# Keys of batches 1 to 3 by stationary sketches in 64x32 tiles, turned in PSUM, with their sums and copies on VectorE

## The chip, the cores and the metric

The kernel runs on one core of a Trainium2 chip. The metric is the device time of one execution in microseconds (us). Nine runs of the kernel before have a median of 267.28 us (266.45 to 270.02). One execution was also profiled: it took 267.74 us, of which the profile's span covers 265.9 us, with TensorE's clock granted in full throughout.

## The reference, cut to what matters

An attention block without softmax is followed by a two-layer network with an exact GELU. For keys and queries, two sketch matrices S1 and S2 (8x32 each) give two vectors of 8 numbers per token, and the features are their outer product, 64 numbers.

```python
def phi(x):
    a = np.einsum('rd,bhsd->bhsr', S1, x)
    b = np.einsum('rd,bhsd->bhsr', S2, x)
    return np.einsum('bhsi,bhsj->bhsij', a, b).reshape(*x.shape[:-1], r * r)
q_p, k_p = (phi(q), phi(k))
kv = np.einsum('bhsf,bhsd->bhfd', k_p, v)
z = np.sum(k_p, axis=2)
num = np.einsum('bhsf,bhfd->bhsd', q_p, kv)
den = np.einsum('bhsf,bhf->bhs', q_p, z)[..., None] + 1e-06
x = num / den            # then heads side by side: 4352 tokens of 128 channels
out = gelu(x @ w_in) @ w_out        # 128 -> 2048 -> 128
```

There are 4 batches, 4 heads, 1088 tokens and a head width of 32. All is float32. Of the tokens of a head, 1024 are the main part and 64 are the remainder.

## The kernel before, in words

The tokens are worked through in chunks: two of 512 tokens per batch (n = 0 to 7) and a last one that holds the 64 remaining tokens of all batches. A chunk needs its batch's `kv` and `z`, so the keys of a whole batch are done ahead of its first chunk. Batch 0 is done at the start, in its own way (`key_features`, `kv_first`), and isn't touched by the diff.

The body is a list of steps, one hidden tile (128 of the 2048 hidden channels of one chunk) per step. In step t, TensorE does the hidden tile (`hidden`, L697), ScalarE its GELU (L704), and TensorE the products with `w_out` of earlier steps (`two_products`, L782). From the third block of chunk 0 on, these use sums of four hidden tiles that GpSimd makes (`token_sums`, L747 to L750: bits_low, bits_a, bits_e, bits_m) and sums of the columns of `w_out` (`channel_sums`, L734 to L737). When a chunk is done, ScalarE and VectorE read its two banks (`drain`, L794 to L803), VectorE combines them (`combine`, L816 to L819), turns the result (L845) and SP stores it.

All other work is hung into steps by hand with `at(t, f, ...)`. Within a step the order is: drains, the hidden tile, token sums, the functions hung there, stores, products. A final loop fixes the order of the text on every engine, so each engine works strictly in that order, and an instruction that waits holds up all behind it on its engine.

For batches 1 to 3 the keys go like this. SP loads a batch's keys with 16 transfers (`load_turned_k`, L108) and its values with one (L100); SP issues all transfers in the order of the text. VectorE turns the keys in blocks of 32x32 (`key_turn_blocks`, L353), two steps ahead of a chunk for batches 2 and 3 (step 30 for batch 2, 62 for batch 3) and at step 14 for batch 1. `features_of_all` has TensorE multiply (`key_products`, L368): blocks of 64 tokens are stationary and the sketches `S12` (32 columns) move, 32 products of 64x64 tiles per batch. ScalarE copies the first factor out of PSUM (`a_t`, L954). `outer_of_all` has VectorE make the features `k_p` (L964). `add_tokens` then adds features of different tokens (L413, L416), for batch 1 on GpSimd and for batches 2 and 3 on VectorE, and for batches 2 and 3 `add_last` adds once more and adds the remainder (L423, L424). `finish_keys` has TensorE make `kv` and `z` (`kv_sum`, L446): 32 products of features and values, 4 for the remainder, and for `z` products with a tile of ones: 4 for batches 2 and 3, and 12 for batch 1 (4 of these with `ones_rem`). These steps are 16, 17 and 21 for batch 1, 38 and 45 for batch 2, 69 and 77 for batch 3.

PSUM has eight banks: two for hidden tiles (`hps`), two for products with `w_out` (`ops`), and two pairs for everything else (`wps`, `work_banks`). A query chunk uses such a pair in the same way as the new keys: `query_sketch` (L584) multiplies stationary sketches in 64x32 tiles with 256 moving columns, and `query_outer` (L596 to L619) turns the result inside PSUM and goes on from there. `attend` (L633) has tiles of the same shape.

Of the kernel before, what the change touches and what calls it, by code (L numbers as in the profile page):

```python
# [8 lines left out]
FP = mybir.dt.float32  # L9
# [7 lines left out]
def kernel(  # L17
# [49 lines left out]
    def work_banks():  # L67

        return wps.tile([128, 2, CW], FP, name="w_ps")
# [4 lines left out]
    def halves(banks):  # L74
        return [banks[:, i] for i in range(2)]
# [23 lines left out]
    def load_main(eng, n, b, heads=slice(0, H)):  # L99
        eng.dma_start(out=main[n, b][:, heads],  # L100
                      in_=src_of[n][b, heads, 0:MAIN, :].rearrange("h (p j) d -> p h j d", j=J))

    def load_turned_k(b):

        src = k[b, :, 0:MAIN, :].rearrange("h (jj t pb jc) d -> h pb t jj (jc d)", jj=4, t=32, pb=4)
        for h in range(H):
            for pb in range(4):
                sp.dma_start(out=main["k", b][pb * 32:(pb + 1) * 32, h].rearrange("t (jj jc) d -> t jj (jc d)", jj=4),  # L108
                             in_=src[h, pb])

    def load_q(n):
        at = n % NCH * CW
# [85 lines left out]
    def load_rest():  # L198

        load_w_out(1, gated=True)  # L200
        for i in range(2, len(pieces)):
            load_w_in(i)
            load_w_out(i)
        for b in range(1, B):
            load_turned_k(b)
            load_main(sp, "v", b)
# [19 lines left out]
    kz_first = big.tile([128, 128], FP, name="kz_first")  # L226

    ones = big.tile([128, D], FP, name="ones")

    ones_rem = big.tile([128, D], FP, name="ones_rem")  # L230
    pool.memset(ones_rem, 0.0)
    pool.memset(ones_rem[:REM], 1.0)
# [113 lines left out]
    def key_turn(b, r, ps, copy, midway=lambda: None):  # L346
        kT[r] = transposed(ps, "kT", [four_tokens("k", b, h, c) for h in (r, r + 2) for c in range(NCH)], copy, midway)

    def key_turn_blocks(b, r):

        kT[r] = att.tile([128, CW], FP, name="kT")
        for i in range(2):
            dve.transpose(out=kT[r][:, i * 256:(i + 1) * 256].rearrange("p (jc jj t) -> p jj jc t", jc=2, jj=4),  # L353
                          in_=main["k", b][:, r + 2 * i].rearrange("p (jj jc) d -> p jj jc d", jj=4))

    def spread(out, a, b):

        n = a.shape[1]
        return dict(out=out, in0=a[:, :, :, None].broadcast_to([128, n, R, R]),
                    in1=b[:, :, None, :].broadcast_to([128, n, R, R]))  # L360

    def key_products(r, banks, col=0):

        for i in range(2 * NCH):
            for c in range(2):
                for t in range(2):
                    at = i * 128 + c * 64
                    pe.matmul(banks[t][c * 64:(c + 1) * 64, col + i * 32:col + (i + 1) * 32],  # L368
                              lhsT=kT[r][t * 64:(t + 1) * 64, at:at + 64],
                              rhs=S12[t * 64:(t + 1) * 64, 2 * t:2 * t + 2].rearrange("p h r -> p (h r)"),  # L370
                              start=True, stop=True)
# [33 lines left out]

    k_s = {}

    def add_tokens(b, r, eng):

        words = mlp.tile([128, LC], U32, name="bits_r")  # L410
        k_s[r] = words.bitcast(FP).rearrange("p (c two one f) -> p c two one f", c=NP, two=2, one=2)
        kp = k_p[b, r].rearrange("p t (c two one) i j -> p t c two one (i j)", c=NP, two=2)
        eng.tensor_add(out=k_s[r].rearrange("p c two one f -> p (c two one f)"),  # L413
                       in0=kp[:, 0].rearrange("p c two one f -> p (c two one f)"),
                       in1=kp[:, 1].rearrange("p c two one f -> p (c two one f)"))
        eng.tensor_add(out=k_s[r][:, :, 0], in0=k_s[r][:, :, 0], in1=k_s[r][:, :, 1])  # L416

    def add_last(b, eng):

        rows = slice(b // 2 * REM, (b // 2 + 1) * REM)  # L420
        for r in range(2):
            to = k_s[r][:, :, 0, 0]
            eng.tensor_add(out=to, in0=to, in1=k_s[r][:, :, 0, 1])  # L423
            eng.tensor_add(out=to[rows], in0=to[rows], in1=k_p_rem[b % 2][rows, r::2].rearrange("p c i j -> p c (i j)"))  # L424

    def flat(features):
        return features.rearrange("p i j -> p (i j)")

# [15 lines left out]
    def kv_product(ps, lhsT, features, h, part, start=False, stop=False):  # L444

        pe.matmul(ps[h * D:(h + 1) * D, part * F:(part + 1) * F], lhsT=lhsT, rhs=features, start=start, stop=stop,  # L446
                  skip_group_check=True)

    def kv_sum(b, ps):


        for i in range(J):
            ch, t, one = i % 2, i // 4, i // 2 % 2
            for h in range(H):
                kv_product(ps, main["v", b][:, h, i, :], flat(k_p[b, h % 2][:, t, h // 2 * 4 + ch * 2 + one]), h, 0,
                           start=i == 0)
# [20 lines left out]
        sketch_of_z(b, banks[:, 0], F)  # L477


    S_abc = [big.tile([128, 2, 2, 2 * R], FP, name=f"S_abc{b}") for b in range(B)]  # L480
    own_r = big.tile([128, 2], FP, name="own_r")

    def spread_sketches():

        pool.tensor_add(out=own_r, in0=mask4[:, 0:2], in1=mask4[:, 2:4])
        own = own_r[:, None, :, None]
        w = S_abc[0]
        pool.memset(w, 0.0)
        pool.tensor_mul(out=w[:, :, :, 0:4], in0=sT[:, 0:R].rearrange("p (i f) -> p i f", i=2)[:, :, None].broadcast_to([128, 2, 2, 4]),
                        in1=own.broadcast_to([128, 2, 2, 4]))  # L490
        pool.tensor_mul(out=w[:, :, :, R:], in0=sT[:, None, None, R:].broadcast_to([128, 2, 2, R]),
                        in1=own.broadcast_to([128, 2, 2, R]))
        for b in range(1, B):
            pool.tensor_copy(out=S_abc[b], in_=w)

# [443 lines left out]
    def at(t, f, *a):  # L939
        slots[t].append(lambda: f(*a))  # L940


    def features_of_all(b):
        banks = halves(work_banks())
        for r in range(2):
            key_products(r, banks, r * 128)
        held["keys"] = banks


        held["factors"] = []  # L950
        for r in range(2):
# [5 lines left out]
    def factors(bank, r):  # L957
        return bank[:, r * 128:(r + 1) * 128].rearrange("p (n r) -> p n r", r=2 * R)

    def outer_of_all(b, adds_by=dve):  # L960
        for r, a in enumerate(held["factors"]):
            k_p[b, r] = att.tile([128, 2, J, R, R], FP, name="k_p")
            for t in range(2):
                dve.tensor_mul(**spread(k_p[b, r][:, t], a[:, t, :, 0:R], factors(held["keys"][t], r)[:, :, R:2 * R]))  # L964
        for r in range(2):
            add_tokens(b, r, adds_by)

    held = {}

# [44 lines left out]
    for n in range(3, NCHUNK):  # L1014

        t = (n - 1) * NF
        b = (n + 1) // 2
        keys = n % 2 and b < B
        if n > 3:
            at(t - 6, query_turn, n)  # L1020
        at(t - 1, attend, n - 1)
        at(t - 1, query_sketch, n)
        at(t - 1, query_outer, n)
        if keys:
            for r in range(2):
# [128 lines left out]
```

## Time and profile before

| | |
|---|---|
| median of nine runs | 267.28 us |
| profiled execution | 267.74 us |
| span of its profile | 265.9 us |
| hidden tiles, L697 | 138.7 us of TensorE |
| GELU, L704 | 73.1 us of ScalarE |
| token sums, L747 to L750 | 143.6 us of GpSimd, 1.3 us each |
| key products of batches 1 to 3, L368 (192 instructions) | 3.4 us of TensorE |
| features of these keys, L964 (12) | 7.4 us of VectorE |
| sums of these keys on VectorE, L413, L416, L423, L424 (16) | 15.4 us |
| sums of batch 1's keys on GpSimd, L413, L416 (4) | 4.0 us |
| turns of these keys, L353 (12) | 4.2 us of VectorE |
| copies of the first factor, L954 (12) | 1.6 us of ScalarE |

Matmuls of TensorE overlap, and busy time counts instructions one by one. A float32 product is recorded as two instructions, so 32 products are x64 in a line of the profile. In the timeline a line gives the start, the length, the engine, the source line, the operation with its tiles, the count, and in brackets the idle time before it with what ended it. In the waits a line gives who waited for what, the sum, the times and the longest.

### The profile page before, as it was taken

To read this page: it belongs to the slowest core of one execution; us is meant where nothing else is said; L and a number is where in the kernel's file an instruction comes from. 1 tells how busy PE (TensorE), PEld (TensorE's weight loads), DVE (VectorE), ACT (ScalarE), POOL (GpSimd) and SP (SyncE) were. 2 spreads that over 40 slices of the span, in tenths; PEclk is the share of its full clock that TensorE was granted. 3 is DMA by queue.
4 is the path that set the end of the run, shared out by engine and by line. 5 is a ranking of instruction groups with operands and counts; after the bars stand their busy time and mean duration, and the time that the engine had idled before them with its cause. 6 is when DMAs were issued, how large, how long until landed. Compare 5 with 4: busy or idle time off the path is not lost.

```text
span 265.9 us, 6138 instructions
## 1 busy us (share of the span) xinstructions
PE 258.7 (97%) x2489; PEld 134.3 (50%) x2489; DVE 147.7 (56%) x315; ACT 118.3 (44%) x239; POOL 169.5 (64%) x180
## 2 busy tenths in 40 slices
PE   8799999999999999999999999999999999999995
PEld 6655444345445454444455554454444454445794
DVE  3776878428499996764085995570456033600140
ACT  5474777433623533353435334533353344433441
POOL 3513006899997875687767877687768776877200
PEclk9999999999999999999999999999999999999999
DMA  6489253525100201102000002002000100020021
GB/s 203 130 249 333 59 171 68 169 63 169 36 7 2 33 10 19 23 0 42 0 2 2 1 2 42 0 1 42 0 0 14 30 2 0 4 38 0 2 35 24
DMA packets 35756, 13.50 MB, mean 51 GB/s; under 512 B 28433, under 2 KB 34321, under 8 KB 35729
## 3 DMA queue, kind: packets, MB, share of 16 engines
q1 hardware_dynamic: 35536, 13.05, 19.5%
q8 instruction: 19, 0.31, 0.4%
q10 hardware_dynamic: 192, 0.07, 0.1%
q14 instruction: 9, 0.07, 0.1%
HBM read 10.88 MB, written 2.23 MB: 49 GB/s over the span
## 4 chain that ended last, share of the span: by engine, by line
PE 66%; SPq 14%; DMA 11%; DVE 6%; issue 2%; POOL 0%; ACT 0%; DVEq 0%; ACTq 0%
PE h_ps L697 31%; PE o_ps L782 28%; SPq L108 7%; DMA v<-in_v_dram 5%; DMA block<-in_moe_w_out_dram 4%; PE w_ps L830 3%; SPq L128 2%; DMA small<-in_moe_w_in_dram 2%; SPq L124 2%; PE w_ps L633 1%; PE w_ps L446 1%; PE w_ps L584 1%; SPq L169 1%; SPq L100 1%; DVE sums L819 1%
## 5 line engine op out<-in xcount | busy, mean ns | idle before, releaser
L697 PE MATMUL h_ps<-xT,w_in 128*64 128x512 f32 (+3 forms) x516 | 138.7, 576 | 0.0
L704 ACT ACTIVATE block<-h_ps 128x512 f32<-128x512 f32 (+1 forms) x128 | 73.1, 571 | 120.1 <-PE h_ps L697 115.8
L782 PE MATMUL o_ps<-block,w_out 128*64 128x256 f32 x224 | 57.8, 380 | 0.0
L697 PEld LDWEIGHTS h_ps<-xT,w_in 128*64 128x64 f32 (+1 forms) x516 | 42.1, 143 | 29.4 <-issue 10.6
L747 POOL TENSOR_TENSOR bits_low<-block 128x512 f32<-128x512 f32 x28 | 35.7, 1274 | 27.0 <-ACT block L704 27.0
L782 PEld LDWEIGHTS o_ps<-block,w_out 128*64 128x64 f32 x224 | 30.1, 137 | 38.7 <-issue 25.5
L748 POOL TENSOR_TENSOR bits_a<-block 128x512 f32<-128x512 f32 x28 | 35.7, 1277 | 13.0 <-ACT block L704 13.0
L749 POOL TENSOR_TENSOR bits_e<-bits_a,block 128x512 f32<-128x512 f32 x28 | 36.3, 1295 | 2.2
L750 POOL TENSOR_TENSOR bits_m<-block,bits_e 128x512 f32<-128x512 f32 x28 | 35.9, 1282 | 2.2
L782 PE MATMUL o_ps<-block,small 128*64 128x256 f32 x112 | 29.1, 383 | 0.6 <-DVE sums L798 0.6
L782 PE MATMUL o_ps<-bits_low,small 128*64 128x256 f32 x112 | 29.2, 383 | 0.0
L782 PE MATMUL o_ps<-bits_a,small 128*64 128x256 f32 x112 | 29.1, 382 | 0.0
L782 PE MATMUL o_ps<-bits_m,w_out 128*64 128x256 f32 x112 | 28.7, 379 | 0.0
L798 DVE TENSOR_TENSOR sums<-o_ps,sums 64x512 f32<-64x512 f32 x8 | 5.5, 682 | 41.6 <-ACT sums L795 24.0
L596 DVE STREAM_TRANSPOSE w_ps<-w_ps 128x512 f32<-128x512 f32 (+1 forms) x7 | 4.8, 686 | 40.6 <-PE w_ps L584 40.6
L782 PEld LDWEIGHTS o_ps<-block,small 128*64 128x64 f32 x112 | 14.7, 137 | 19.9 <-issue 10.3
L782 PE MATMUL o_ps<-bits_e,small 128*64 128x256 f32 x112 | 17.2, 385 | 0.6 <-POOL bits_e L749 0.6
L833 PE MATMUL o_ps<-g,w_out 128*128 128x512 f32 x32 | 16.4, 600 | 0.1
L782 PEld LDWEIGHTS o_ps<-bits_m,w_out 128*64 128x64 f32 x112 | 15.3, 137 | 0.0
L782 PEld LDWEIGHTS o_ps<-bits_a,small 128*64 128x64 f32 x112 | 14.8, 137 | 0.0
L782 PEld LDWEIGHTS o_ps<-bits_low,small 128*64 128x64 f32 x112 | 14.7, 137 | 0.0
L782 PEld LDWEIGHTS o_ps<-bits_e,small 128*64 128x64 f32 x112 | 7.4, 136 | 11.5 <-issue 8.5
(186 smaller groups left out, 307.0 us busy)
## 6 DMA issues: line engine op xcount, KB each, us to landing
block<-in_moe_w_in_dram SPq DMA_DIRECT2D x3, 512.0 KB, 8.1
block<-in_moe_w_out_dram SPq DMA_DIRECT2D x3, 512.0 KB, 10.9
k<-in_k_dram SPq DMA_DIRECT2D x48, 32.0 KB, 1.8
v<-in_v_dram SPq DMA_DIRECT2D x3, 512.0 KB, 4.2
q<-in_q_dram SPq DMA_DIRECT2D x24, 64.0 KB, 3.4
out_dram<-oT SPq DMA_DIRECT2D x24, 64.0 KB, 2.2
k<-in_k_dram SPq DMA_DIRECT2D x2, 256.0 KB, 3.0
q<-in_q_dram SPq DMA_DIRECT2D x2, 256.0 KB, 5.0
```

The lines of the kernel that those rows point to most:

```text
L108: sp.dma_start(out=main["k", b][pb * 32:(pb + 1) * 32, h].rearrange("t (jj jc) d -> t jj (jc d)", jj=4), in_=src[h, pb])
L124: sp.dma_start(out=q_rem[h * 32:(h + 1) * 32, b % 2, b // 2], in_=q[b, h, MAIN:S, :].rearrange("(n t) d -> t n d", t=32))
L697: pe.matmul(ps[rows, :W], lhsT=w[:, rows], rhs=xT[n][:, :W], start=True, stop=True)
L704: act.activation(out=g_of[n, fi][:, :W], in_=ps[:, :W], func=ACT.Gelu)
L747: pool.tensor_sub(out=s[3], in0=a11, in1=a21)
L748: pool.tensor_add(out=s[1], in0=a21, in1=a22)
L749: pool.tensor_sub(out=s[2], in0=s[1], in1=a11)
L750: pool.tensor_sub(out=s[4], in0=a12, in1=s[2])
L782: pe.matmul(acc[n][bank][half * 64:(half + 1) * 64, col:col + HW], lhsT=fixed, rhs=moving, start=opens and e == 0 and name in "4715", stop ...
L798: dve.tensor_add(out=C[lo, 1], in0=a1[lo], in1=C[lo, 0])
L830: pe.matmul(o_of[n][i][:, :128], lhsT=g[:, i * 128:(i + 1) * 128], rhs=w_tile(w_out_sb, fi), start=first, stop=final)
L833: pe.matmul(o_of[n], lhsT=w_tile(w_out_sb, fi), rhs=g, start=first, stop=final)
```

## The change

The keys of batches 1 to 3 lie differently in SBUF: 32 partitions per head, 32 tokens in each, so that 4 transfers load a batch, and the values are loaded to match with 4 transfers. VectorE turns the keys with two instructions of 128x512. For batch 2 this is now done at step 28, for batch 3 it stays at 62. A new constant `S_ab` holds both sketches for the two heads of a tile's 64 rows, made by GpSimd at step 11. `features_of_all` now has 8 products with `S_ab` stationary and 256 key columns moving. The rest is VectorE's: it turns the result inside PSUM, copies the first factor, makes the features in two instructions of 1024 elements, sums the 8 tokens of a partition with two reduces (reading with a step of 128 elements and writing to PSUM), and makes `k_s` by a copy of one half of the rows and an addition of the remainder's features on the other half. The remainder is so in `k_s` for batch 1 as well, `ones_rem` goes, and every batch has 4 products for `z`. `add_tokens` for batch 1 is at step 17, for batches 2 and 3 in the step of the features.

```diff
-    def load_turned_k(b):
-        src = k[b, :, 0:MAIN, :].rearrange("h (jj t pb jc) d -> h pb t jj (jc d)", jj=4, t=32, pb=4)
+    def load_keys(b):
         for h in range(H):
-            for pb in range(4):
-                sp.dma_start(out=main["k", b][pb * 32:(pb + 1) * 32, h].rearrange("t (jj jc) d -> t jj (jc d)", jj=4),
-                             in_=src[h, pb])
+            sp.dma_start(out=main["k", b][h * 32:(h + 1) * 32].rearrange("t x j d -> t (x j d)"),
+                         in_=k[b, h, 0:MAIN, :].rearrange("(t n) d -> t (n d)", t=32))
+
+    def load_values(b):
+        src = v[b, :, 0:MAIN, :].rearrange("h (t q n) d -> q t h (n d)", t=32, q=4)
+        for g in range(4):
+            sp.dma_start(out=main["v", b][g * 32:(g + 1) * 32].rearrange("t h n d -> t h (n d)"), in_=src[g])
...
-    def key_turn_blocks(b, r):
-        kT[r] = att.tile([128, CW], FP, name="kT")
-        for i in range(2):
-            dve.transpose(out=kT[r][:, i * 256:(i + 1) * 256].rearrange("p (jc jj t) -> p jj jc t", jc=2, jj=4),
-                          in_=main["k", b][:, r + 2 * i].rearrange("p (jj jc) d -> p jj jc d", jj=4))
+    def key_turn_blocks(b, x):
+        kT[x] = att.tile([128, CW], FP, name="kT")
+        dve.transpose(out=kT[x], in_=main["k", b][:, 2 * x:2 * x + 2].rearrange("p x j d -> p (x j d)"))
...
-        if b == 1:
-            for h in range(H):
-                kv_product(ps, ones_rem, flat(k_p_rem[b][:, h]), h, 1)
-        for m in range(2 if b == 1 else 1):
-            for h in range(H):
-                kv_product(ps, ones, k_s[h % 2][:, h // 2, 0, m], h, 1, stop=b > 1 or m == 1)
+        for h in range(H):
+            kv_product(ps, ones, k_s[b][:, h], h, 1, stop=True)
...
+        pool.tensor_mul(out=S_ab, in0=sT[:, None].broadcast_to([128, 2, 2 * R]), in1=own_r[:, :, None].broadcast_to([128, 2, 2 * R]))
...
     def features_of_all(b):
-        banks = halves(work_banks())
-        for r in range(2):
-            key_products(r, banks, r * 128)
-        held["keys"] = banks
-        held["factors"] = []
-        for r in range(2):
-            a = att.tile([128, 2, J, 2 * R], FP, name="a_t")
-            for t in range(2):
-                act.copy(out=a[:, t, :, 0:R], in_=factors(banks[t], r)[:, :, 0:R])
-            held["factors"].append(a)
+        ps = work_banks()
+        for g in range(4):
+            for c in range(NP):
+                rows = slice(c * 64, (c + 1) * 64)
+                pe.matmul(ps[g * 32:(g + 1) * 32, c, :CW // 2], lhsT=S_ab[rows].rearrange("p r x -> p (r x)"),
+                          rhs=kT[g // 2][rows, g % 2 * 256:(g % 2 + 1) * 256], start=True, stop=True)
+        held["keys"] = ps
...
+    def outer_of_all(b):
+        ps = held["keys"]
+        tok = ps[:, :, CW // 2:]
+        dve.transpose(out=tok, in_=ps[:, :, :CW // 2])
+        x = tok.rearrange("p c (k x) -> p c k x", x=2 * R)
+        a = att.tile([128, NP, 2 * J, R], FP, name="a_t")
+        dve.tensor_copy(out=a, in_=x[:, :, :, 0:R])
+        k_p[b] = []
+        for c in range(NP):
+            features = att.tile([128, J, 2, F], FP, name="k_p")
+            dve.tensor_mul(out=features.rearrange("p n r (i j) -> p (n r) i j", i=R),
+                           in0=a[:, c, :, :, None].broadcast_to([128, 2 * J, R, R]),
+                           in1=x[:, c, :, None, R:].broadcast_to([128, 2 * J, R, R]))
+            k_p[b].append(features)
+
+    def add_tokens(b):
+        sums = held["keys"][:, :, :2 * F]
+        for c in range(NP):
+            dve.tensor_reduce(out=sums[:, c], in_=k_p[b][c].rearrange("p n r f -> p (r f) n"), axis=mybir.AxisListType.X,
+                              op=AX.add)
+        k_s[b] = att.tile([128, H, F], FP, name="k_s", bufs=1)
+        to = k_s[b].rearrange("p (c r) f -> p c (r f)", c=NP)
+        rows, rest = (slice(x * REM, (x + 1) * REM) for x in (b // 2, 1 - b // 2))
+        dve.tensor_copy(out=to[rest], in_=sums[rest])
+        dve.tensor_add(out=to[rows], in0=sums[rows], in1=k_p_rem[b % 2][rows].rearrange("p (c r) i j -> p c (r i j)", c=NP))
...
-    at(16, outer_of_all, 1, pool)
+    at(16, outer_of_all, 1)
     at(16, turn_keys_rem, 1)
     at(17, features_rem, 1)
+    at(17, add_tokens, 1)
...
-                at(t - 2, key_turn_blocks, b, r)
+                at(t - 2 if n > 3 else t - 4, key_turn_blocks, b, r)
...
-            at(t + 6, add_last, b, dve)
+            at(t + 5 + (n == NCH + 1), add_tokens, b)
```

More of the change, by code (lines that the diff above doesn't have):

```diff
@@ L204, in load_rest @@
         for b in range(1, B):
-            load_turned_k(b)
-            load_main(sp, "v", b)
+            load_keys(b)
+            load_values(b)
             for c in range(NCH):
@@ L228 @@
     ones = big.tile([128, D], FP, name="ones")
-    ones_rem = big.tile([128, D], FP, name="ones_rem")
-    pool.memset(ones_rem, 0.0)
-    pool.memset(ones_rem[:REM], 1.0)
     v_rem_aug = [big.tile([128, H, D if b else 2 * D], FP, name=f"v_rem_aug{b}") for b in range(B)]
@@ L406 @@
     k_s = {}
[L408 to L420, printed above, removed]
-        for r in range(2):
-            to = k_s[r][:, :, 0, 0]
-            eng.tensor_add(out=to, in0=to, in1=k_s[r][:, :, 0, 1])
-            eng.tensor_add(out=to[rows], in0=to[rows], in1=k_p_rem[b % 2][rows, r::2].rearrange("p c i j -> p c (i j)"))
     def flat(features):
@@ L452, in kv_sum @@
         for i in range(J):
-            ch, t, one = i % 2, i // 4, i // 2 % 2
             for h in range(H):
-                kv_product(ps, main["v", b][:, h, i, :], flat(k_p[b, h % 2][:, t, h // 2 * 4 + ch * 2 + one]), h, 0,
-                           start=i == 0)
+                kv_product(ps, main["v", b][:, h, i, :], k_p[b][h // 2][:, i, h % 2], h, 0, start=i == 0)
         for h in range(H):
             kv_product(ps, v_rem_aug[b][:, h, :], flat(k_p_rem[b % 2][:, h]), h, 0, stop=True)
-        if b == 1:
-            for h in range(H):
-                kv_product(ps, ones_rem, flat(k_p_rem[b][:, h]), h, 1)
-        for m in range(2 if b == 1 else 1):
-            for h in range(H):
-                kv_product(ps, ones, k_s[h % 2][:, h // 2, 0, m], h, 1, stop=b > 1 or m == 1)
+        for h in range(H):
+            kv_product(ps, ones, k_s[b][:, h], h, 1, stop=True)
     kv_T = {}
@@ L477, in turn_kv @@
         sketch_of_z(b, banks[:, 0], F)
+    S_ab = big.tile([128, 2, 2 * R], FP, name="S_ab")
     S_abc = [big.tile([128, 2, 2, 2 * R], FP, name=f"S_abc{b}") for b in range(B)]
@@ L943, in features_of_all @@
     def features_of_all(b):
-        banks = halves(work_banks())
-        for r in range(2):
-            key_products(r, banks, r * 128)
-        held["keys"] = banks
-        held["factors"] = []
-        for r in range(2):
-            a = att.tile([128, 2, J, 2 * R], FP, name="a_t")
-            for t in range(2):
-                act.copy(out=a[:, t, :, 0:R], in_=factors(banks[t], r)[:, :, 0:R])
-            held["factors"].append(a)
-    def factors(bank, r):
-        return bank[:, r * 128:(r + 1) * 128].rearrange("p (n r) -> p n r", r=2 * R)
@@ L960, in outer_of_all @@
[L960 to L966, printed above, removed]
+        ps = work_banks()
[4 more added lines that the diff above has]
+                          rhs=kT[g // 2][rows, g % 2 * 256:(g % 2 + 1) * 256], start=True, stop=True)
```

## The prediction

> **What bounds the kernel now.** I read the busy table first, then the chain that ended last, then the waits of TensorE, then the timeline around the edited steps.
>
> ```profile
> PE 258.7 (97%) x2489; PEld 134.3 (50%) x2489; DVE 147.7 (56%) x315; ACT 118.3 (44%) x239; POOL 169.5 (64%) x180
> ```
>
> TensorE is busy for 258.7 of 265.9 us. By stretches, nearly all that is missing lies before 25 us and after 250 us, which the diff doesn't touch. In between there are two gaps, and TensorE's waits name them:
>
> ```profile
> PE o_ps L782 <- POOL bits_e L749: 0.6, 1, 0.6
> PE o_ps L782 <- DVE sums L798: 0.6, 1, 0.6
> ```
>
> So time is gained in two ways only: less TensorE work, and these two gaps. The chain that ended last gives the pace, as start, length and work. From 87 us on it is TensorE without a break:
>
> ```profile
> 104.37 0.59 PE w_ps L633 x16
> 104.96 0.43 PE w_ps L584 x16
> ...
> 141.44 0.86 PE h_ps L697 x4
> 142.30 1.07 PE w_ps L368 x64
> 143.36 1.01 PE h_ps L697 x4
> ```
>
> A hidden tile costs 0.86 us. The old key products (L368) cost 1.07. Eight products of 64x32 tiles over 256 columns (L584) cost 0.43 behind others of the same tile shape, and 0.59 is the cost of such a set (L633) behind another shape. The hidden tile behind L368 takes 1.01: changing the shape costs 0.15 to 0.16.
>
> The gaps are a little longer than the view of waits says. The timeline of TensorE, GpSimd and VectorE there:
>
> ```profile
> 54.32 0.29 PE L446 MATMUL w_ps<-k_p_rem,ones_rem 128*32 128x64 f32 x8
> 54.43 0.41 PE L446 MATMUL w_ps<-bits_r,ones 128*32 128x64 f32 x16
> 54.51 1.27 POOL L747 TENSOR_TENSOR bits_low<-block 128x512 f32<-128x512 f32 x1
> 57.10 1.27 POOL L749 TENSOR_TENSOR bits_e<-bits_a,block 128x512 f32<-128x512 f32 x1
> 57.41 0.38 PE L782 MATMUL o_ps<-bits_low,small 128*64 128x256 f32 x1
> 58.42 0.65 PE L782 MATMUL o_ps<-bits_e,small 128*64 128x256 f32 x4 [0.63 <-POOL bits_e L749]
> ...
> 73.45 1.41 DVE L353 STREAM_TRANSPOSE kT<-k 128x256 f32<-128x256 f32 x4
> 85.40 0.71 DVE L845 STREAM_TRANSPOSE oT<-sums 128x512 f32<-128x512 f32 x1
> 86.60 0.68 DVE L798 TENSOR_TENSOR sums<-o_ps,sums 64x512 f32<-64x512 f32 x1 [0.49 <-ACT sums L795]
> ```
>
> Gap one: a pair started at 57.41, pairs follow each other by 0.21, so the next was due at 57.62 and came at 58.42: 0.80 us. GpSimd was late because it summed batch 1's keys from 48.66 to 52.77 (L413 and L416), then did channel sums, and so began the token sums only at 54.51, though ScalarE had finished their block at 52.14. Gap two: the hidden tile at 85.66 should take 1.01, and the next product came at 87.34 instead of 86.67: 0.67 us. It waited for the drain of chunk 1, at the end of an unbroken VectorE chain that runs from 70.53 and holds the four turns of batch 2's keys.
>
> [...] for contiguous inputs: 285 ns for 128 elements (L605) and 228 for 64 (L501), a slope of 0.9 ns and about 0.17 us fixed. [...] batch 3's sums (L413) took 1.43 and 1.76 us with GpSimd busy, and one took 0.78 at 93.67. [...] No row of this trace has such a read, and the change's reduce is one: it steps 128 words (512 bytes) from token to token.
>
> **The change part by part.**
>
> TensorE, keys: 32 products of 64 keys by 32 sketch columns become 8 with the sketches stationary and 256 columns moving, the shape of L633 and L584. 1.07 to 0.59 saves 0.48 per batch, 1.44 over three. Batch 1's sums for z: 12 products become 4. In 54.32 to 54.77 lie 24 instructions (two per product) and one change of shape, 0.45 - 0.15 = 0.30, so 16 fewer save 0.20. Batches 2 and 3 keep four.
>
> GpSimd: the four sums of batch 1 leave it (4.0 us). Its channel sums then run behind L290, which ends at 47.83, and are done by 49.7; the token sums start when the block is complete, near 51.7, and bits_e is ready near 55.5. Gap one goes: -0.80. The added S_ab product is about 0.2 us at 23 us, in front of GpSimd's idle 15.8 us.
>
> ScalarE: twelve a_t copies of 223 ns go. They were hidden; worth nothing.
>
> Queue: 16 key transfers of a batch become 4, and one value transfer becomes four: SP issues 27 fewer (about 0.6 us each). All of these data landed well before their use (batch 1's turns at 42.24 show no wait), so nothing; q and the remainders come earlier, also unused.
>
> VectorE, turns: two of 128x512 at 0.70 (as L535) for four at 0.35, the same 1.4 us. For batch 2 they move from step 30 to 28, in front of the drain, where VectorE stands idle for 3.48 us (67.05 to 70.53); batch 2's keys, issued by 48.2, are there. The chain to L798 gets shorter by 1.33 (73.45 to 74.78) and TensorE arrives 0.48 earlier, so 0.85 is to be had and 0.67 needed: gap two goes, with only 0.18 to spare.
>
> VectorE, batches 2 and 3: the old work after the drain ran 8.52 us (89.51 to 98.03) and 11.66 (145.25 to 156.91). The new: transposition 0.73, copy 0.43, products 2.35, two reduces 2R, copy and sum 0.85, with waits some 4.5 + 2R. With R below 2 it is no longer than before. Needed by 99.9 and 157.4: hidden.
>
> VectorE, batch 1, is where it turns. Before, GpSimd's sums were ready at 52.77 and used at 54.43. Now VectorE does everything in a row, and the products for z (step 21) wait for it, with the rest of TensorE's queue behind them. From the end of L535 at 46.91: transposition to 47.64; copy of 128x256 at 0.43 (as L679) to 48.10; two products of 1024 elements, the elements for which four of L964 took 2.48, at 2.35 to 50.5; the remainder's product 0.41 to 50.85; two reduces; copy and sum at 0.42 each. With the waits between: 51.8 + 2R, and 0.05 until TensorE sees it. TensorE is at its z products at 54.32 - 0.48 = 53.84. The stall is S = 2R - 2.0.
>
> R, 1024 elements behind 0.17 us fixed[...] I take 1.94[...]. Before z nothing else waits: the slot for kv's bank is the one of the remainder's keys, free at 50.85. After it, GpSimd is ready.
>
> Sum: -1.44 - 0.20 - 0.80 - 0.67 + 1.9 = -1.2 us. On the profiled execution, 267.74 (span 265.9 and 1.8 around it), this is 266.5; that execution lies 0.46 above the median of nine, 267.28, from which I get 266.1.
>
> **The rivals.** A measurement of this kernel can tell about 0.5%, 1.34 us, from no change.
>
> First, the forecast: [...] 266.1, alone 265.3 to 266.9. Chance 0.45, of which 0.20 beyond 0.5% faster.
>
> Second, the reduce reads at the full rate: S is 0.5 and the sum -2.6, 264.7. [...] Chance 0.27, 0.23 of it faster.
>
> Third, the reduce takes 2.3 to 2.7 us: the stall of 2.6 to 3.4 eats the gain, 266.8 to 267.6. [...] Chance 0.18, 0.06 of it slower by its upper tail.
>
> Fourth, the other side: the reduce is so slow that it decides alone. It cancels the gain at R = 2.55 and makes 0.5% slower at R = 3.23. At 4 ns per element R is 4.3, S 6.6 and the sum +3.5 (270.8), and VectorE would then be late for z in batches 2 and 3 too (13.1 us from 89 and 145 us, past the time of use): 271 or more. [...] Chance 0.06.
>
> Fifth, the change moves work that was not felt: gap two stays [...] (0.18 to spare), and a small wait appears: 266.7. Chance 0.04, within 0.5%.
>
> **How the numbers follow.** Faster 0.20 + 0.23 = 0.43; within 0.5% 0.25 + 0.04 + 0.12 + 0.04 = 0.45; slower 0.06 + 0.06 = 0.12. The range leaves out the fourth and the tails of the second and third: 264.0 to 268.2.
>
> **What would show it.** The key products near 0.59 instead of 1.07 at about 84 and 142 us. The TENSOR_REDUCE of 128x1024 near 1.94 us: this one row decides between the cases. A TensorE wait on VectorE's k_s near 55 us, of 2R - 2.0. No wait on bits_e after it, and none at the start of chunk 2's products. GpSimd's first token sums near 52 instead of 54.51. The prediction is wrong if k_s is ready before TensorE comes, if gap two stays, or if another wait of over 0.5 us appears, first of all at the z products of batch 2 or at the turns moved in front of the drain.

## The result, and the profile after

The changed kernel takes 265.46 us, the median of 17 runs (264.93 to 265.87), against 267.03 us for the kernel before, the median of 52 runs, the nine shown first among them: a ratio of 0.9934, 95% interval 0.9918 to 0.9949. It is 1.6 us faster. Its profiled execution took 265.19 us with a span of 263.4 us.

Of the 2.5 us between the two profiled spans, 1.04 lie ahead of the first changed product: batch 1's key set starts at 45.43 us before and at 44.39 us after. In the execution before, TensorE waited 1.42 us at 12.55 us for a transfer of queries, which is issued ahead of all that the diff touches. Of the twelve other profiled executions in this study, eleven have this key set at 44.2 to 44.9 us, whichever kernel they start from, and one at 46.55. So this part is a difference between executions. From the first key product to the end of the span it is 220.5 us before and 219.0 us after, -1.5 us, and this agrees with the medians. All sums below are of this stretch.

The row of the busy table that answers to the one shown of before:

```profile
PE 256.8 (97%) x2329; PEld 132.0 (50%) x2329; DVE 150.7 (57%) x305; ACT 116.8 (44%) x227; POOL 165.2 (63%) x175
```

TensorE is still what bounds the kernel, with 160 instructions fewer. Its waits have changed places. The waits of TensorE in the changed kernel:

```profile
PE w_ps L426 <- DVE k_s L955: 1.6, 1, 1.6
PE w_ps L840 <- PEq L1128: 0.8, 1, 0.8
PE h_ps L654 <- DVE x_tok L646: 0.4, 1, 0.4
```

The waits on bits_e and on the drain's sums are gone. A new one, longer than either, stands at the products for z of batch 1. The other two lie near the ends of the span and were there before. The chain that ended last, around batch 3's keys (start, length, work):

```profile
139.19 0.86 PE h_ps L673 x4
140.05 0.59 PE w_ps L925 x16
140.64 1.01 PE h_ps L673 x4
```

The key set takes 0.59 us where it took 1.07, and the hidden tile behind it 1.01 as before.

The timeline of VectorE, GpSimd and TensorE around batch 1's keys, where the new wait arises:

```profile
45.80 0.68 DVE L933 STREAM_TRANSPOSE w_ps<-w_ps 128x512 f32<-128x512 f32 x1
46.52 0.42 DVE L936 COPY a_t<-w_ps 128x256 f32<-128x256 f32 x1
46.98 2.35 DVE L940 TENSOR_TENSOR k_p<-a_t,w_ps 128x1024 f32<-128x1024 f32 x2
49.25 0.41 DVE L402 TENSOR_TENSOR k_p_rem<-a_rem,w_ps 128x256 f32<-128x256 f32 x1
49.58 4.05 DVE L949 TENSOR_REDUCE w_ps<-k_p 128x128 f32<-128x1024 f32 x2
49.84 1.27 POOL L723 TENSOR_TENSOR bits_low<-block 128x512 f32<-128x512 f32 x1 [1.16 <-ACT block L680]
52.44 1.27 POOL L725 TENSOR_TENSOR bits_e<-bits_a,block 128x512 f32<-128x512 f32 x1
52.70 0.29 PE L426 MATMUL w_ps<-k_p_rem,v_rem_aug 128*32 128x64 f32 x8
53.67 0.43 DVE L954 COPY k_s<-w_ps 64x256 f32<-64x256 f32 x1
54.11 0.42 DVE L955 TENSOR_TENSOR k_s<-w_ps,k_p_rem 64x256 f32<-64x256 f32 x1
54.58 0.32 PE L426 MATMUL w_ps<-k_s,ones 128*32 128x64 f32 x8 [1.59 <-DVE k_s L955]
57.68 0.60 PE L758 MATMUL o_ps<-bits_e,small 128*64 128x256 f32 x4
```

VectorE works from 45.80 to 54.53 us with pauses of no more than 0.05 us, and nearly half of it is the two reduces. TensorE has done the remainder's products (52.70) and would start the products for z at 52.82, as in the kernel before such a group starts 0.11 us behind the other (54.32 and 54.43); they start at 54.58, 1.76 us late. GpSimd now waits for ScalarE, not ScalarE's blocks for GpSimd, and bits_e is ready at 53.7, four microseconds before its use at 57.68, which shows no wait.

The timeline around batch 2's keys and the drain of chunk 1:

```profile
66.17 1.26 DVE L352 STREAM_TRANSPOSE kT<-k 128x512 f32<-128x512 f32 x2
...
83.80 0.66 PE L925 MATMUL w_ps<-kT,S_ab 64*32 64x256 f32 x16
83.82 0.68 DVE L774 TENSOR_TENSOR sums<-o_ps,sums 64x512 f32<-64x512 f32 x1 [1.26 <-ACT sums L771]
84.39 1.08 PE L673 MATMUL h_ps<-xT,w_in 128*64 128x512 f32 x4
85.30 0.38 PE L758 MATMUL o_ps<-block,small 128*64 128x256 f32 x1
```

The turns are now done at 66.17, and the drain's reading (L774) is over at 84.50, before TensorE comes for the bank at 85.30. Last, the groups of the new work on VectorE (busy time, then the mean of one in ns, then idle time before):

```profile
L949 DVE TENSOR_REDUCE w_ps<-k_p 128x128 f32<-128x1024 f32 x6 | 12.0, 1992 | 0.2
L940 DVE TENSOR_TENSOR k_p<-a_t,w_ps 128x1024 f32<-128x1024 f32 x6 | 7.1, 1218 | 0.1
```

A reduce of 1024 elements takes 1992 ns, 1.6 times the product of 1024 elements.

Taken stage by stage, from start to start on TensorE:

| stage | before, us | after, us | difference | predicted |
|---|---|---|---|---|
| key set, batch 1 | 1.07 | 0.59 | -0.48 | -0.48 |
| from there to batch 1's kv | 6.79 | 6.80 | 0 | 0 |
| batch 1's kv and z, to the next hidden tile | 1.48 | 3.05 | +1.57 | +1.7 |
| on to the first products with bits_e (gap one) | 3.65 | 2.85 | -0.80 | -0.80 |
| on to batch 2's key set | 26.17 | 26.12 | -0.05 | 0 |
| key set, batch 2 | 1.07 | 0.59 | -0.48 | -0.48 |
| on to batch 2's kv (gap two) | 13.17 | 12.20 | -0.97 | -0.67 |
| key set, batch 3 | 1.06 | 0.59 | -0.47 | -0.48 |
| from TensorE's last product to the end of the span, with the last store | 3.57 | 3.77 | +0.20 | 0 |

Between batch 2's kv and batch 3's key set lie 43.39 us in both. The last row is not a chance difference between two executions: from batch 3's key set on, every profile of a kernel that starts from the changed one takes 0.16 to 0.19 us longer than every one that starts from the kernel before. Where it comes from is open.

### The profile page after: what moved, and what is told of

It reads as the page before. It is cut to its first block, busy times and chain, and to the rows that moved or that the text cites. A ratio compares the mean times of both kernels' runs of the same rounds, so it can differ in the third digit from the quotient of the medians.

```text
span 263.4 us, 5751 instructions
## 1 busy us (share of the span) xinstructions
PE 256.8 (97%) x2329; PEld 132.0 (50%) x2329; DVE 150.7 (57%) x305; ACT 116.8 (44%) x227; POOL 165.2 (63%) x175
## 4 chain that ended last, share of the span: by engine, by line
PE 81%; SPq 6%; DVE 5%; DMA 5%; issue 1%; ACT 0%; POOL 0%; DVEq 0%
PE h_ps L673 37%; PE o_ps L758 33%; DMA block<-in_moe_w_out_dram 4%; PE w_ps L806 3%; SPq L121 2%; DVE w_ps L949 2%; PE w_ps L609 1%; PE w_ps L840 1%; PE w_ps L560 1%; SPq L132 1%; PE w_ps L426 1%; SPq L181 1%; DVE k_p L940 1%; SPq L113 1%; SPq L106 1%
## 5 line engine op out<-in xcount | busy, mean ns | idle before, releaser
L723 POOL TENSOR_TENSOR bits_low<-block 128x512 f32<-128x512 f32 x28 | 35.7, 1273 | 29.8 <-ACT block L680 29.8
L774 DVE TENSOR_TENSOR sums<-o_ps,sums 64x512 f32<-64x512 f32 x8 | 5.5, 683 | 41.2 <-ACT sums L771 23.6
L680 ACT ACTIVATE g<-h_ps 128x512 f32<-128x512 f32 x16 | 9.6, 597 | 7.5 <-PE h_ps L673 6.8
```

The costliest lines, as they stand in the source:

```text
L680: act.activation(out=g_of[n, fi][:, :W], in_=ps[:, :W], func=ACT.Gelu)
L723: pool.tensor_sub(out=s[3], in0=a11, in1=a21)
L774: dve.tensor_add(out=C[lo, 1], in0=a1[lo], in1=C[lo, 0])
```

## The experiments

Two questions were open: whether the reduce is slow because of its step, and what each part of the change is worth by itself. Ratios are to the kernel before, on the same chip.

| run | kernel | median, us | ratio, 95% interval |
|---|---|---|---|
| 1 | after, reduces read contiguously | 264.02 | 0.9883 (0.9844 to 0.9923) |
| 2 | before, batch 2's turns at 28 | 265.87 | 0.9946 (0.9925 to 0.9966) |
| 3 | before, batch 1's sums on VectorE | 266.55 | 0.9977 (0.9948 to 1.0006) |
| 4 | after, query turns behind the token sums | 264.79 | 0.9904 (0.9868 to 0.9940) |
| 5 | 4, with batch 1's recovery later as well | 264.31 | 0.9907 (0.9882 to 0.9931) |
| 6 | after, key products twice | 266.18 | 0.9977 (0.9963 to 0.9990) |
| 7 | before, key products twice | 268.56 | 1.0064 (1.0050 to 1.0079) |
| 8 | after, eight reduces added in idle time | 265.70, one time | |
| 9 | before with both moves, 2 and 3 | 265.10 | 0.9924 (0.9903 to 0.9945) |
| 10 | after, beside 9 and 11 | 265.25 | 0.9936 (0.9913 to 0.9959) |
| 11 | 5 again | 263.97 | 0.9882 (0.9859 to 0.9904) |
| 12 | after, batch 2's turns back at 30 | 266.97 | 0.9991 (0.9974 to 1.0008) |

### 1. The reduce without its step

```diff
-            dve.tensor_reduce(out=sums[:, c], in_=k_p[b][c].rearrange("p n r f -> p (r f) n"), ...
+            dve.tensor_reduce(out=sums[:, c], in_=k_p[b][c].rearrange("p n r f -> p (n r f)").rearrange("p (f n) -> p f n", n=J), ...
```

> The kernel after, with the two reduces of each batch reading the same number of elements in the order in which they lie (groups of 8 neighbours, so not the tokens' sums; z is left out in this sense) instead of at a step of 128. Theory (the step makes the read slow, and the reduce sets the wait for z): a reduce takes about 1.25 us instead of 2.0, TensorE's wait for k_s shrinks from 1.6 to under 0.3, and the time falls by 1.3 to 1.6 us against the kernel after, to about 264.0, ratio 0.988. Rival (a reduce of 1024 elements into PSUM in groups of 8 costs 2 us in any order): reduce and wait stay, time as the kernel after, 265.5, ratio 0.993 to 0.994.

The reduces' group in this run:

```profile
L949 DVE TENSOR_REDUCE w_ps<-k_p 128x128 f32<-128x1024 f32 x6 | 7.4, 1226 | 0.2
```

This kernel adds neighbouring features where the tokens of one feature should be added, so it leaves out the right `z`; its work is otherwise the same. The order of reading alone takes a reduce from 1992 to 1226 ns, and the view of waits lists none on k_s any more. The products for z still start 0.31 us behind the remainder's, where 0.11 would do, so 0.2 us of the delay is left. The stretch from the first key product on is 217.4 us instead of 219.0. So the step costs 0.77 us a reduce, and through the wait 1.4 us (by the ratios) to 1.6 us (by the stretch) of the kernel. The theory held.

### 8. Which steps are slow

In the last chunk, where VectorE stands idle, eight reduces of the same 1024 elements were added; six write to SBUF and two to PSUM. They change nothing that the kernel computes.

```diff
+    def read_steps():
+        k = k_p[3][0].rearrange("p n r f -> p (n r f)")
+        to = big.tile([128, 2 * F], FP, name="read_to")
+        for s in (1, 2, 4, 16, 64, 128):
+            dve.tensor_reduce(out=to.rearrange("p (a s) -> p a s", s=s), in_=k.rearrange("p (a n s) -> p a s n", n=J, s=s), ...
+        bank = work_bank()
+        for s in (1, 128):
+            dve.tensor_reduce(out=bank[:, :2 * F].rearrange("p (a s) -> p a s", s=s), in_=k.rearrange("p (a n s) -> p a s n", n=J, s=s), ...
...
+    at(119, read_steps)
```

> The kernel after, with eight more reduces of 128x1024 in groups of 8 on VectorE while it stands idle late in the kernel (step 119), reading one tile of features at steps of 1, 2, 4, 16, 64 and 128 elements into SBUF, then 1 and 128 into PSUM; nothing uses their results. Theory [...]: steps 1 and 2 take 1.23 us, 4 and more take 2.0, and the target makes no difference. Rival (only large steps are slow): step 4 and 16 at 1.2 to 1.5. Rival (the slow rate needs no more than a single word between neighbours): step 2 at 2.0 already.

VectorE's timeline in eight views, each from a later start, so that each line begins with the next reduce. The differences of the first column are the reduces one by one, in the order of the loop; where the place of the result changes, the length of a line with x1 is taken, since the next reduce starts a little before the last one ends:

```profile
227.44 10.52 DVE L963 TENSOR_REDUCE read_to<-k_p 128x128 f32<-128x1024 f32 x6
228.68 9.28 DVE L963 TENSOR_REDUCE read_to<-k_p 128x128 f32<-128x1024 f32 x5
229.93 8.03 DVE L963 TENSOR_REDUCE read_to<-k_p 128x128 f32<-128x1024 f32 x4
232.03 5.93 DVE L963 TENSOR_REDUCE read_to<-k_p 128x128 f32<-128x1024 f32 x3
233.95 4.00 DVE L963 TENSOR_REDUCE read_to<-k_p 128x128 f32<-128x1024 f32 x2
235.96 2.00 DVE L963 TENSOR_REDUCE read_to<-k_p 128x128 f32<-128x1024 f32 x1
237.88 3.22 DVE L967 TENSOR_REDUCE w_ps<-k_p 128x128 f32<-128x1024 f32 x2
239.13 1.97 DVE L967 TENSOR_REDUCE w_ps<-k_p 128x128 f32<-128x1024 f32 x1
```

Steps of 1 and 2 words take 1.24 and 1.25 us. Steps of 4, 16, 64 and 128 words take 2.10, 1.92, 2.01 and 2.00 us. Into PSUM it is 1.25 for step 1 and 1.97 for step 128, so at these two steps the place of the result plays no part. Once the step is four words, how far it goes makes little difference. The times that the theory gave held. Those of both rivals did not: step 4 takes 2.10 us and step 16 1.92, not 1.2 to 1.5, and step 2 takes 1.25, not 2.0. The dearest step here, 2.10 us, is 1.9 ns per element if 0.17 us of it are fixed, an estimate from the prediction's two short reduces (L605 and L501). What makes four words dear and two not, no run shows.

### 4, 5 and 11. The new wait, from its other side

If the wait on k_s is what costs, it can be taken away without touching the reduce, by starting VectorE's chain earlier or asking for its result later. Run 4 moves chunk 2's query turns behind the token sums.

```diff
-    at(15, query_turn, 2)
     at(16, features_of_all, 1)
...
     at(17, add_tokens, 1)
+    at(17, query_turn, 2)
```

> The kernel after, with the turn of chunk 2's queries (0.70 us of VectorE at step 15) put behind batch 1's sums. Theory (TensorE waits for k_s at the end of one VectorE chain, so whatever is taken from in front of it comes off the wait): k_s 0.65 us earlier, wait 1.6 to about 0.95, time 264.8, ratio 0.991. Rival (the chain starts with TensorE's products, or the sketches of chunk 2 then wait for the turn): less than 0.2 us gained, 265.4, ratio 0.9935.

TensorE's wait in this run, from the view of waits:

```profile
PE w_ps L426 <- DVE k_s L955: 1.0, 1, 1.0
```

The transposition of the sketches now starts 0.79 us after the start of the key set, not 1.41, and the rest of the chain follows it. The stage of kv and z takes 2.44 us, not 3.05, and the stretch 218.4 us, not 219.0: as expected.

Run 5 moves batch 1's recovery one step later as well.

```diff
-    at(21, finish_keys, 1)
-    at(22, lambda: turn_kv(1, held["kv"]))
+    at(22, finish_keys, 1)
+    at(23, lambda: turn_kv(1, held["kv"]))
```

> The kernel after, with the turn of chunk 2's queries behind batch 1's sums and batch 1's kv and z one step later (step 22, its turn at 23). Theory (the wait for k_s is the only thing that batch 1 still costs, and 0.86 us of hidden tile put in front of z hides it): wait near 0.1 instead of 1.6, and what follows from z (copy, turn, sketch of z) is still in time for the sketches of step 24; 263.9 to 264.1, ratio 0.988. Rival (the chain from z to the sketches of step 24 becomes the wait): TensorE waits at step 24 for what is saved at z, 264.8 as with the turn moved alone, ratio 0.991.

TensorE and VectorE there:

```profile
53.97 0.42 DVE L955 TENSOR_TENSOR k_s<-w_ps,k_p_rem 64x256 f32<-64x256 f32 x1
...
54.09 0.29 PE L426 MATMUL w_ps<-k_p_rem,v_rem_aug 128*32 128x64 f32 x8
...
54.44 0.32 PE L426 MATMUL w_ps<-k_s,ones 128*32 128x64 f32 x8
```

TensorE takes up k_s as it becomes ready, and no wait is listed; the stage takes 1.5 us. The stretch is 217.5 us, 1.5 below the changed kernel, yet the median of six runs, 264.31, was above what was expected. So the pair was measured once more, beside the changed kernel.

> The changed kernel as it is, on the same chip as the two beside it: 265.4, ratio 0.993 to 0.994. Theory: level with the two small edits alone, within 0.3 us. Rival: over 0.7 us below them, if the key products kept more of their gain than the stages show.

> The changed kernel with the query turns behind the token sums and with batch 1's recovery and turns later (the pair of moves tried before), on the same chip: theory, with the wait for the token sums gone and no new one, 1.3 to 1.6 us below the changed kernel, 263.8 to 264.1, ratio 0.988. Rival: only what the query turns alone gave, 0.6 us, ratio 0.991.

Measured were 265.25 and 263.97 us: 1.3 us apart, ratio 0.9882. This is as good as the contiguous reduce of run 1 (0.9883), with the slow reduce in place and nothing left out. No other full kernel of this study is faster.

### 2, 3 and 9. The two small edits without the new key products

Run 2 takes the kernel before and moves only batch 2's turns; run 3 only gives batch 1's sums to VectorE; run 9 does both.

```diff
-                at(t - 2, key_turn_blocks, b, r)
+                at(t - 2 if n > 3 else t - 4, key_turn_blocks, b, r)
```

> The kernel before, with only batch 2's turns moved from step 30 to 28. Theory (gap two, 0.67 us before chunk 2's first products, comes from the turns in VectorE's chain): the gap goes, 0.5 to 0.7 us less than before, 266.4, ratio 0.9975. Rival (the chain is held by something else, and the turns only change place): no wait goes, 267.0, ratio 1.000.

The wait on the sums is gone, and from the hidden tile behind batch 2's key set to its kv it is 12.20 us instead of 13.17. The direction was as expected, the size 0.97 instead of 0.5 to 0.7. The median fell by more, 1.3 us, but its interval reaches from 0.9 to 2.0 us and the whole stretch is 1.0 us shorter, so only the 0.97 is shown.

```diff
-    at(16, outer_of_all, 1, pool)
+    at(16, outer_of_all, 1)
```

> The kernel before, with batch 1's four sums on VectorE instead of GpSimd. Theory (gap one, 0.80 us before the bits_e products, comes from these sums in GpSimd's queue, and VectorE has the time for them): the gap goes, the sums are ready near 52.5 and z doesn't wait, 0.6 to 0.8 us less, 266.3, ratio 0.997. Rival (GpSimd is late for another reason, or VectorE becomes late for z): a wait of the same size stays or comes at the z products, 267.0 or more, ratio 1.000.

The wait on bits_e is gone and the stage of gap one takes 2.85 us instead of 3.65, just as in the changed kernel. In total it is 266.55 us, near what was expected, though the interval includes 1 and the stage alone carries the reading.

> The kernel before with two edits and no new key products: batch 2's turns at step 28, and batch 1's feature sums on VectorE. Each edit alone took away one wait on TensorE: 0.97 us of stage for the turns, 0.80 us for the sums. Theory (the two gaps are separate, and the new key products' gain is about eaten by the wait for the token sums): the gaps add up, -1.8 us, 265.2 to 265.4, ratio 0.993 to 0.994, that is, these two edits give the whole gain of the change. Rival (one gap takes up what the other gives back): only about -1 us, 266.0 or more, ratio 0.996 or above.

All of TensorE's waits in run 9:

```profile
PE w_ps L864 <- PEq L1138: 0.8, 1, 0.8
PE h_ps L678 <- DVE x_tok L670: 0.4, 1, 0.4
```

Nothing but the two waits of the span's ends. The gaps add up: 218.7 us from the first key product on, against 220.5. The median of 265.10 us stands 0.15 below the changed kernel's on the same chip (265.25), with intervals that overlap for the most part. Two small edits, a step number and the engine of four sums, do with the old key products all that the change does.

### 12. The change without its move

```diff
-                at(t - 2 if n > 3 else t - 4, key_turn_blocks, b, r)
+                at(t - 2, key_turn_blocks, b, r)
```

> The changed kernel with batch 2's turns back at step 30: only the move is undone. Theory (VectorE's chain through the turns and the drain keeps its length, and TensorE comes to the hidden tile behind the shorter key set 0.48 us earlier): the wait on the drain's sums comes back and is longer by those 0.48, so 0.97 + 0.48 = 1.4 us are lost against the changed kernel, 266.6 to 266.8, ratio 0.998 to 0.999, and the key set's gain in batch 2 counts for nothing without the move. Rival (the whole chain moves with TensorE): only the old gap comes back, 0.97 us, 266.2, ratio 0.997. Rival (the gap had gone through the fewer and larger turns anyway): no wait, 265.3, ratio 0.9935.

TensorE's waits in this run, and its timeline at the drain of chunk 1:

```profile
PE w_ps L426 <- DVE k_s L955: 1.6, 1, 1.6
PE o_ps L758 <- DVE sums L774: 1.0, 1, 1.0
```

```profile
86.55 1.08 PE L673 MATMUL h_ps<-xT,w_in 128*64 128x512 f32 x4
...
87.91 0.68 DVE L774 TENSOR_TENSOR sums<-o_ps,sums 64x512 f32<-64x512 f32 x1 [0.49 <-ACT sums L771]
88.64 0.43 PE L758 MATMUL o_ps<-block,small 128*64 128x256 f32 x1 [1.02 <-DVE sums L774]
```

The products behind the hidden tile start 2.09 us after it, where the changed kernel needs 0.91. To batch 2's kv it is 13.59 us instead of 12.20, +1.39; the stretch is 220.4 us, +1.4. The gap has grown by 0.42 us, nearly the 0.48 that the key set saves, as the theory had it: VectorE's chain begins with the drain of chunk 0, ahead of batch 2's key set, and doesn't get shorter when that set does. Without the move the change is worth 0.09 us, ratio 0.9991, which can't be told from nothing.

### 6 and 7. The price of the key products

Each kernel's key products twice over, into the same bank, show where their time counts.

```diff
-        for g in range(4):
+        for g in list(range(4)) * 2:
```

> The kernel after, with the eight key products of each batch made twice (the same values into the same place). Theory (TensorE sets the time behind batch 1, and a set costs 0.43 us behind one of its own shape; in batch 1 TensorE waits for VectorE's k_s anyway, which doesn't become later): 0.86 us more than the kernel after, two times 0.43 and nothing for batch 1, 266.3, ratio 0.997. Rival (the time of the key products isn't felt, the gain is all from the two gaps): 265.5, ratio 0.994.

```diff
-        for r in range(2):
+        for r in (0, 1, 0, 1):
             key_products(r, banks, r * 128)
```

> The kernel before, with the 32 key products of each batch made twice. Theory: a set costs 0.93 us behind its own shape (64 instructions by 14.5 ns). Batch 1: 0.93, since GpSimd's sums and with them gap one become later too. Batch 2: the products lie ahead of gap two, which takes up some 0.7 to 0.9 of them, so 0.0 to 0.2. Batch 3: 0.93. Together 1.9 to 2.1 us more than before, 269.0, ratio 1.0075. Rival (the key products aren't felt): as before, 267.0. Rival (no gap takes anything up): 2.8 us more, 269.9, ratio 1.0105.

The sets of batch 2 in the timelines of TensorE, first the new products (run 6), then the old ones (run 7):

```profile
83.69 1.09 PE L925 MATMUL w_ps<-kT,S_ab 64*32 64x256 f32 x32
```

```profile
84.55 2.07 PE L368 MATMUL w_ps<-S,kT 64*64 64x32 f32 x128
```

Start to start the new set takes 1.03 instead of 0.59, +0.43, and the old one 2.00 instead of 1.07, +0.93. In run 6 batch 1's 0.43 goes into the wait on k_s, which falls to 1.1 us, and batches 2 and 3 pay theirs in full: the stretch is 219.9 us, 0.8 above the changed kernel's, and the median 266.18 us is near the 266.3 expected. In run 7 batch 2's 0.93 goes into gap two, and batches 1 and 3 pay theirs in full: 268.56 us, +1.8 of the 2.8 us of work added. So in these two runs time on TensorE counted only where no wait followed that took it up.

## Why the prediction came out as it did

Predicted were 266.1 us and -1.2 us, measured 265.46 us and -1.6 us, inside the likeliest case's own range of 265.3 to 266.9. The ratio puts it 0.66% below the kernel before, past the 0.5% that the prediction takes for the least that can be told; it had given 0.43 to that and 0.45 to less. By its steps:

**Key products, -1.44: right.** Measured -0.48, -0.48 and -0.47.

**Products for z, -0.20: right.** The stage of kv and z grew by 1.57 us, the delay in it is 1.76: -0.19. From the first product for z to the next hidden tile it was 0.45 us (54.32 to 54.77) and is 0.25 (54.58 to 54.83).

**Gap one, -0.80: right,** in the changed kernel and in run 3 alone. GpSimd's first sums start at 49.84 us, which is 50.9 in the time of before, even earlier than the 52 expected: bits_low needs only the first and third of the block's four tiles, not the complete block that the prediction waits for. Behind the gap another 0.05 us went, the slower start that is described under gap two.

**Gap two, -0.67: the mechanism right, the size off.** This is the term of the sum that was mis-sized. It measured 0.97 us, in the changed kernel and in run 2 with the old key products alike. Two parts were missed. The prediction took the hidden tile's 1.01 us from the chain and the start from the timeline. In the timeline the products follow at 0.91 us (84.39 to 85.30), so the gap itself was 0.77. And the drain holds TensorE a second time. VectorE and TensorE's loading of weights (PEld) behind the gap, in the kernel before:

```profile
89.17 0.42 DVE L803 TENSOR_TENSOR sums<-o_ps,sums 64x256 f32<-64x256 f32 x1
89.64 0.13 PEld L782 LDWEIGHTS o_ps<-block,w_out 128*64 128x64 f32 x1 [0.81 <-DVE sums L803]
```

The products with `w_out` that follow the next hidden tile start here, 0.05 us after the drain's last addition has ended, and 0.96 us behind that tile; in the changed kernel it is 0.86. That is 0.10 us. Another 0.10 are the first pairs of products behind the two waits, 0.26 us each where 0.21 is usual. Runs 3 and 12, which have the first wait, have all of this too, and no run without it has any. That the move would be enough was right, but not by the margin worked out. The prediction had 0.18 us to spare; L774 ends at 84.50 and TensorE comes at 85.30, 0.80 later. The combination of chunk 0, in the same chain, is why. VectorE and GpSimd there, in the kernel before:

```profile
81.07 1.18 DVE L816 TENSOR_TENSOR sums<-sums 64x256 f32<-64x256 f32 x1
82.06 1.34 POOL L749 TENSOR_TENSOR bits_e<-bits_a,block 128x512 f32<-128x512 f32 x1
82.27 1.41 DVE L817 TENSOR_TENSOR sums<-sums 64x256 f32<-64x256 f32 x1
```

And in the changed kernel:

```profile
78.96 0.73 DVE L792 TENSOR_TENSOR sums<-sums 64x256 f32<-64x256 f32 x1
79.71 0.42 DVE L793 TENSOR_TENSOR sums<-sums 64x256 f32<-64x256 f32 x1
79.85 1.41 POOL L724 TENSOR_TENSOR bits_a<-block 128x512 f32<-128x512 f32 x1 [0.44 <-ACT block L680]
```

These two additions read both inputs from SBUF. Each of the two long ones ends 0.27 to 0.28 us after the GpSimd instruction beside which it began (L748, to 81.98, and L749, to 83.40). So does the first one after (0.28 us behind L723, which ends at 79.41), but there little of that instruction was left; then GpSimd pauses for ScalarE, and the second addition, begun in the pause, takes 0.42 us although GpSimd starts again beside it. Together they take 1.15 us instead of 2.59. The fourteen profiles of this study hold 224 of these additions. Of 99 that begin while a GpSimd instruction runs, 98 end 0.27 to 0.29 us after it, whether 0.2 or 1.2 us of it were left; the 125 others take 0.37 to 0.42. The drain's additions (L801 to L803 and their like), which read one input from PSUM, take 0.41 to 0.43 us in all 336 cases, 258 of them begun beside a GpSimd instruction. So by these traces an addition of this kind doesn't run slowly beside GpSimd: its time is that of a wait for the instruction that GpSimd has begun.

The two are short as well in run 9, but long in run 2 (1.26 and 1.41), which has the move without the lighter GpSimd, and in run 12, where the chain is later (1.26 and 1.40). In run 2 the drain is done 0.52 us before TensorE comes, and in the changed kernel TensorE comes 0.48 earlier. With long additions some 0.04 us would have been left, an estimate from these two numbers. So the margin of 0.80 was luck: it hung on how two engines fell beside each other, and was not foreseen.

**The new wait, +1.9: right.** The row that was to decide between the cases shows 1992 ns for 1940. That alone would make the wait 2.0 us; VectorE's chain was some 0.2 us shorter than worked out, counted from the key set, and the wait came to 1.76. That these two misses partly cancel is luck. The 1940 ns, like the rivals' lengths of the reduce, was the author's estimate: the trace of the kernel before has no reduce that steps. It was chosen because this one steps far, and run 8 shows that distance isn't what costs: a step of 16 words takes 1.92 us, one of 128 takes 2.00. The size was right, the reason for it only in part.

**What was costed at nothing** was so: no wait on a_t copies or on a load, and batches 2 and 3 have k_s ready at 95.2 and 151.5 us, used from 97.6 and 154.7 us on. Not foreseen were 0.2 us more at the end, with the last store.

**The sum:** -1.43 - 0.19 - 0.80 - 0.05 - 0.97 + 1.76 + 0.20 = -1.48, the -1.5 of the profiled stretch. Of the 0.64 us between forecast and result, 0.25 is the kernel before, whose median was 267.28 us in the nine runs shown first and 267.03 in those beside the changed kernel; 0.30 is gap two.

**The rivals:** the reduce at full rate (264.7 us) fell by the row of L949. What it would have given, run 1 shows: 264.0. A reduce of 2.3 us and more, and the side where it decides alone, fell by the same row. The fifth, that gap two stays, fell, but it was close to a right warning: the two additions of the chain, held up by GpSimd, took 2.59 us before and, held up less, 1.15 after. That is a larger difference than the margin of 0.80, and it happened to help. Run 12 shows what was at stake: where the gap comes back, it takes the gain whole.

What the prediction's sum held but its words didn't say is the split. The new key products with all that belongs to them earn 1.62 us on TensorE and pay 1.76 for the wait they bring; the two gaps are the result.

## What to carry to other kernels

Take a gain on the bounding engine as real only after looking at what that engine waits for next: here 0.48 us saved in front of a wait was worth next to nothing until the wait's own cause was moved. Price a reduction by the order in which it reads (here 1226 ns contiguously and 1992 at a step of 128), and when its result is late, look first for other work ahead of it on the same engine and for a later place of its use; moving three calls gave here what a faster reduce would have given. Look past the first wait for others on the same work: the drain held TensorE twice. And read both ends of a gap from the same view.

## What the runs showed of the hardware that was not expected

A float32 tensor_reduce of 1024 elements per partition on VectorE takes 1.24 us at a step of one word and 1.25 at a step of two, and 1.92 to 2.10 us at steps of 4 to 128 words, with nearly the same times into PSUM (run 8). This was found for one input in SBUF; into PSUM only steps of 1 and 128 were run. At both gaps a wait on TensorE cost 0.05 us beyond its length: the first pair of products behind it took 0.26 us instead of 0.21, at gap two twice. Why was not tried. And an addition of 64x256 elements with both inputs in SBUF waited for the GpSimd instruction that was running when it began, and ended 0.27 to 0.29 us after it (98 of 99 cases, taking 0.49 to 1.46 us). Begun while GpSimd was idle, it took 0.37 to 0.42 us, even where GpSimd started beside it, and with one input in PSUM it took 0.41 to 0.43 us whatever GpSimd did.
